# Score visits of three pieces in a PE-bound attention and MLP kernel: two single PSUM banks serve as a third strip

## The chip, the cores and the metric

The kernel runs on one core of one Trainium2 chip. The metric is the device time in microseconds of one execution. Of the core's engines five matter here: TensorE (PE), VectorE (DVE), ScalarE (ACT), GpSimd (POOL) and SyncE (SP), which issues most of the DMAs. PE writes its results to PSUM[...]; one bank holds 512 fp32 values for each of 128 partitions. ACT and DVE read PSUM; before PE may write a bank again, its reader has to be done.

## The reference

Causal attention with 16 beacon keys in front, and then an MLP with squared ReLU on the joined heads. B = 8 batches, H = 8 heads, S = 576 tokens, D = 64; d_model = 512, d_ff = 2048.

```python
k_all = concat([beacon_k, k], axis=2);  v_all = concat([beacon_v, v], axis=2)   # 16 + 576 keys
scores = q @ k_all.T / sqrt(64)          # a later key (not a beacon) is masked
a = softmax(scores)                      # + 1e-9 in the denominator
attn = a @ v_all                         # B, H, S, D
x = attn.transpose(0, 2, 1, 3).reshape(4608, 512)
h = x @ w_in;  g = relu(h) ** 2;  out = g @ w_out
```

## The kernel before

**Attention.** Heads are worked on in pairs, four pairs in a batch. The causal scores of one pair, keys on the partitions, are laid out as a stream of 1664 columns; the four pairs of a batch make 6656 columns, cut into 13 *pieces* of 512 (`PIECES`). A piece is computed in a double-bank *strip*: one bank for the even head, one for the odd head (`emit_scores`, L611, matmuls with a 64-row contraction). One ACT instruction of 2 x 512 columns turns a strip into exponentials in `pt` (`add_exp`, L620). DVE masks the diagonal blocks of a whole pair (L689, L693). Then PE multiplies by the values (L715, 15 matmuls of 65 columns for one head: 64 values and a sum), and DVE divides by the sum (L732 takes the reciprocal, L734 multiplies) into `xn`. `xn` is transposed into `xT`, by PE in the first three batches (L782) and by DMA in the others (L765). Batch 0 is done in smaller parts; batches 1 to 7 go through `add_batch`.

**MLP.** Tokens are taken in nine chunks of 512 (`add_chunk`). The first layer is 16 groups of four 512-column matmuls (L878); ACT or DVE applies the ReLU (L894 or L896) out of PSUM, and DVE squares two groups at once (L903). The second layer makes 128 tokens at a time with 16 matmuls of 512 columns (L916); ACT or DVE copies the bank to `osb` (L316 or L318), and SP stores it.

**PSUM.** Two strips of two banks, and four single banks `ps0` to `ps3` for all else: first- and second-layer groups, L715, transposes.

**Order.** Nothing is left to a scheduler of the compiler. `Order.run` is a planner: it plays the engines forward in time with assumed durations, gives each free engine the available operation of the lowest `prio`, hands out strips and single banks from pools, and returns them when their reader has ended in its account. The instructions are then emitted in that order; semaphores are derived from what each instruction reads and writes. `gate_at` holds the visits back until enough of the MLP has been done.

**A visit** is one run of score matmuls of PE. `new_visit` opens it and `add_batch` puts two pieces into it, so a batch has seven visits: six of two pieces and one of one piece. A visit of two takes both strips.

**The last 128 tokens.** `add_last` makes the second layer of the last 128 tokens in three groups of 256, 128 and 128 output columns (L828), each with its own bank, copy and store; the last copy is of 128 columns on ACT, and ACT also issues the last store.

Of the kernel before, what the change touches and what calls it, by code (L numbers as in the profile page):

```python
# [9 lines left out]
FP32 = mybir.dt.float32  # L10
# [6 lines left out]
class Op:  # L17
# [1 line left out]

    __slots__ = ("name", "engs", "dur", "emit", "prio", "need", "users", "left", "ready",  # L20
                 "take", "give", "gate", "held", "slots", "dma", "pe_time", "behind", "followers",
                 "sync", "insts", "late")

    def __init__(self, name, engs, dur, emit, prio=0.0, deps=(), take=None, give=None,
                 gate=None, dma=0.0, pe_time=0.0, behind=(), sync=(), late=0.0):
        self.name = name
        self.late = late
        self.engs = engs if isinstance(engs, (tuple, list)) else (engs,)
        self.dur = dur
        self.emit = emit  # L30
        self.prio = prio
        self.sync = list(sync)
        self.need = list(deps) + self.sync
        self.users = []
        self.take = (*take, 1)[:3] if take else None
        self.give = give
        self.gate = gate
        self.held = None
        self.slots = []
        self.dma = dma  # L40
        self.pe_time = pe_time
        self.behind = list(behind)
        self.followers = []


class Order:
# [3 lines left out]
    LAT = {"PE": 0.2, "ACT": 0.2, "DVE": 0.15, "POOL": 0.25, "SP": 0.1, "-": 0.0}  # L50

    FILL_UNTIL = 22.0
    DEPTH = {"SP": 4, "ACT": 8, "POOL": 8}
    DMA_LAT = {"SP": 0.6, "ACT": 0.6, "POOL": 2.0}

# [13 lines left out]
    def run(self):  # L69
# [24 lines left out]
        while events:  # L94
            now = events[0][0]
            while events and events[0][0] <= now + 1e-9:
                _, _, kind, op = heapq.heappop(events)
                if kind in ("done", "done_pe"):
                    for u in op.users:
                        if ("PE" in u.engs) == (kind == "done_pe"):  # L100
                            u.left -= 1
                            if u.left == 0:
                                release(u)
                elif kind == "give":
                    from_op, which = op.give if isinstance(op.give, tuple) else (op.give, 0)
                    pool, cls = from_op.take[:2]
                    self.pools[pool].append(from_op.slots[which])
                    if cls in self.inuse:
                        self.inuse[cls] -= 1
            again = True  # L110
            while again:
                again = False
                for e in engines:
                    if free[e] > now + 1e-9:
                        continue
                    best = None
                    fallback = None
                    for op in avail[e]:
                        if any(free[x] <= now + 1e-9 for x in op.engs[:op.engs.index(e)]):
                            continue  # L120
                        if op.take:
                            pool, cls, need = op.take
                            if len(self.pools[pool]) < need:
                                continue
                            if cls in self.limits and self.inuse[cls] + need > self.limits[cls]:
                                continue
                        if op.gate is not None and not op.gate(self):
                            if fallback is None or op.prio < fallback.prio:
                                fallback = op
                            continue  # L130
                        if op.dma and len(lanes[e]) >= self.DEPTH[e] and lanes[e][-self.DEPTH[e]] > now + 1e-9:
                            continue
                        if best is None or op.prio < best.prio:
                            best = op
# [17 lines left out]
                        avail[ee].remove(op)  # L152
                    if op.take:
                        pool, cls, need = op.take
                        op.slots = [self.pools[pool].pop(0) for _ in range(need)]
                        op.held = (pool, cls, op.slots[0])
                        if cls in self.inuse:
                            self.inuse[cls] += need
# [35 lines left out]
def kernel(  # L194
# [75 lines left out]
    rcp = [sb(f"rcp{i}", [128, 2 * NT], FP32) for i in range(4)]  # L270
    tri = sb("tri", [128, 4, 128], BF16)
    strips = [psum.tile([128, 2, 512], FP32, name=f"strip{i}") for i in range(2)]
    ps = [psum.tile([128, 512], FP32, name=f"ps{i}") for i in range(4)]

    def wait_for(later, first):
        tc.add_manual_dep(later.ins, first.ins.name, mybir.DependencyInfo(
# [338 lines left out]
                    start=True, stop=True,  # L615
                )

    def add_exp(name, qk, s, at, width, prio):
        def emit(e):
            nc.scalar.activation(pt[:, :, at:at + width], strips[qk.slots[s]][:, :, 0:width],  # L620
                                 AF.Exp, bias=0.0, scale=scale)

        return add(name, "ACT", 0.18 + 2 * width / 1200.0, emit, prio=prio, deps=[qk], give=(qk, s))

    exps_of = {}
    CROSS = ()
    SHIFT = 0.25
    opened = []

    def new_visit(b, n):  # L630
        pos = HP * b + 512.0 * n / PW
        parts = []

        def emit(e):
            for s, (bb, m) in enumerate(parts):
                emit_scores(bb, PIECES[m], strips[qk.slots[s]])

        qk = add(f"qk{b}.{n}", "PE", 0.2, emit, prio=100.0 * pos - 1000.0, take=("strip", "strip"), gate=gate_at(pos - SHIFT))
        opened.append((qk, parts))

    def add_batch(b):
        for pr in range(HP):
            p = HP * b + pr
            qk_ops[p], av_ops[p], exps_of[p] = [], [], []
        for n in range(NPC):
            if not opened:
                new_visit(b, n)
            qk, parts = opened[0]
            parts.append((b, n))
            qk.take = ("strip", "strip", len(parts))  # L650
            qk.dur += sum(t1 - t0 for _, _, t0, t1, _ in PIECES[n]) / 2400.0
            pairs = sorted({mm[0] for mm in PIECES[n]})
            e = add_exp(f"exp{b}.{n}", qk, len(parts) - 1, 512 * n, 512,
                        1.0e-2 * (HP * b + 512.0 * n / PW) - 30.0)
            for pr in pairs:
                p = HP * b + pr
                for o in deps_of(b, pr, 0) + av_ops[p - HP]:
                    if o not in qk.need:
                        qk.need.append(o)
                qk_ops[p].append(qk)  # L660
                exps_of[p].append(e)
            if len(parts) == 2 or n == NPC - 1 and b not in CROSS:
                opened.clear()
        for pr in range(HP):
            add_phase(b, pr, HP * b + pr, 0, WHOLE[pr][0], 100.0 * (HP * b + pr), exps_of[HP * b + pr])

    def add_pair(b, pr):
        p = HP * b + pr
        qk_ops[p], av_ops[p] = [], []
        for n, ph in enumerate(SPLIT):  # L670
            base = 20.0 * RANK.index((p, n))
            exps = []
            for i, (mms, off, width) in enumerate(ph.pieces):
# [3 lines left out]
                qk = box["qk"] = add(f"qk{p}.{n}.{i}", "PE", 0.2 + sum(max(96, mm[2] - mm[1]) for mm in mms) / 2400.0, emit_qk,  # L677
                                     prio=base + i - 1000.0, deps=deps_of(b, pr, n), take=("strip", "strip"))
                qk_ops[p].append(qk)
                exps.append(add_exp(f"exp{p}.{n}.{i}", qk, 0, PW * p + off, width, (base + i) * 1.0e-4 - 400.0))  # L680
            add_phase(b, pr, p, n, ph, base, exps)

    def add_phase(b, pr, p, n, ph, base, exps):
# [133 lines left out]
                    in_=moe_w_out.rearrange("(c p) f -> p c f", p=128)[:, i * n:(i + 1) * n, :])]  # L817
            w_ops["out", i] = add(f"wout{i}", "POOL", 1.3, emit, prio=-90 + i, behind=[v_loads[1][4]] if i == 0 else [w_ops["out", i - 1]], dma=2.6)

    def add_last(j, ts, base, sq):  # L820
        u = 2 * NCH - 1
        for n, (lo, hi) in enumerate(((0, 256), (256, 384), (384, 512))):
            prev, box = None, {}
            for qd in range(4):
                def emit_s2(e, qd=qd, lo=lo, hi=hi, box=box):
                    o = ps[box["s2"].held[2]][:, 0:hi - lo]
                    for fc in range(4 * qd, 4 * qd + 4):
                        nc.tensor.matmul(o, G_of(j)[:, fc, ts * 128:(ts + 1) * 128],  # L828
                                         w_out_sb[:, fc, lo:hi], start=(fc == 0), stop=(fc == NFT - 1))

                prev = add(f"s2.{j}.{ts}.{qd}.{n}", "PE", 0.865 * (hi - lo) / 512, emit_s2,
                           prio=base + 100 + 4 * ts + n + 0.1 * qd,
                           deps=sq[2 * qd] + sq[2 * qd + 1] + [w_ops["out", qd]], behind=[o for o in (prev or s2_ops.get((j, ts)),) if o],
                           take=None if qd else ("ps", "mlp"), pe_time=0.865 * (hi - lo) / 512)
                box.setdefault("s2", prev)
            s2_ops[j, ts] = prev
            e_ = ("ACT", "DVE", "ACT")[n]

            def emit_ev(e, lo=lo, hi=hi, box=box):
                copy_on(e, osb[u % 2][:, ts % 2, lo:hi], ps[box["s2"].held[2]][:, 0:hi - lo])  # L840

            ev = add(f"ev{j}.{ts}.{n}", e_, 0.15 + (hi - lo) / 1100.0, emit_ev, prio=-15.0, deps=[prev] + st_ops[u - 2], give=box["s2"])

            def emit_st(e, n=n, lo=lo, hi=hi):
                t0 = u * 256 + 128 * (ts % 2)
                (nc.sync, nc.sync, nc.scalar)[n].dma_start(out=out[t0:t0 + 128, lo:hi], in_=osb[u % 2][:, ts % 2, lo:hi])

            st_ops[u].append(add(f"st{j}.{ts}.{n}", ("SP", "SP", "ACT")[n], 0.65, emit_st, prio=-20.0, deps=[ev], dma=0.2))

    def G_of(j):  # L850
        return g[j % 2]

    def add_chunk(j):
        base = 1.0e5 + 1000.0 * j
        G = g[j % 2]
# [49 lines left out]
                sqs.append(add(f"sq{j}.{f}.{n}", "DVE", 0.1 + 0.6 * N / TCH, emit_sq, prio=-10.0, deps=relus))  # L905
            sq.append(sqs)
        for ts in range(TCH // 128):
            if j == NCH - 1 and ts == TCH // 128 - 1:
                add_last(j, ts, base, sq)
                continue  # L910
            prev, first = None, {}
            for qd in range(4):
                def emit_s2(e, ts=ts, qd=qd, first=first):
# [134 lines left out]
```

The softmax here doesn't subtract the row's maximum and nothing guards it: scores larger than these inputs give would overflow.

## Time and profile before

| | us |
|---|---|
| median of 3 runs (lowest to highest) | 341.09 (340.71 to 342.69) |
| profiled execution, its own time | 342.69 |
| its span, first to last instruction | 341.0 |
| PE busy | 335.6 |
| ACT busy | 190.3 |
| DVE busy | 173.0 |
| POOL busy | 92.5 |
| HBM traffic | 37.22 MB read, 9.44 MB written |

The granted TensorE clock was full (1.00) throughout. The profile is one execution; its span leaves out 1.7 us of the execution's own time around the first and last instruction. A row of PE covers a pipelined matmul with a modelled end, so rows overlap: the spacing of the starts tells what a matmul costs, not the length of its row. PE's attention work ends at 263 us or so; after that only the MLP is left.

### The profile page before, as it was taken

The numbers are of one execution on the slowest core, as the hardware profiler recorded it, in microseconds if no ns is written. First come the engines' busy times: TensorE is split into PE (matmuls) and PEld (weight loads), VectorE is DVE, ScalarE is ACT, GpSimd is POOL, SyncE is SP. The second block draws the span as 40 slices with busy tenths as digits, with TensorE's granted clock in tenths as the row PEclk, the third lists the DMA queues.
The fourth block names the chain that finished last, engine by engine and source line by source line (L and its number), as shares of the span: only waits on it lengthen the run. The fifth ranks groups of instructions, "written<-read, shape, count | busy, mean of one in ns | idle before, by whom it ended". The sixth has DMA issues, their size and how long they took to land.

```text
span 341.0 us, 7787 instructions
## 1 busy us (share of the span) xinstructions
PE 335.6 (98%) x3197; PEld 187.4 (55%) x3197; DVE 173.0 (51%) x389; ACT 190.3 (56%) x270; POOL 92.5 (27%) x145
## 2 busy tenths in 40 slices
PE   8999999999999999999999999999999999999996
PEld 7677665544564555555467855545454544444444
DVE  3886886238465982477336743767255502401400
ACT  2886765367647765576456653675367316514721
POOL 9773712406504533042315041504000000000000
PEclk9999999999999999999999999999999999999999
DMA  8999987999999999799989998997310131011003
GB/s 143 209 185 213 209 149 165 224 241 217 170 204 238 219 172 189 162 238 188 201 154 220 226 215 131 217 233 125 105 62 2 29 104 62 0 60 65 0 2 123
DMA packets 143953, 51.72 MB, mean 152 GB/s; under 512 B 130702, under 2 KB 138798, under 8 KB 143918
## 3 DMA queue, kind: packets, MB, share of 16 engines
q1 hardware_dynamic: 135375, 42.19, 61.8%
q0 software_dynamic: 7904, 8.69, 15.0%
q8 instruction: 25, 0.41, 0.5%
q10 hardware_dynamic: 639, 0.36, 0.4%
q14 instruction: 10, 0.08, 0.1%
HBM read 37.22 MB, written 9.44 MB: 137 GB/s over the span
## 4 chain that ended last, share of the span: by engine, by line
PE 97%; DVE 1%; issue 0%; ACT 0%; DVEq 0%
PE ps L878 36%; PE ps L916 36%; PE ps L715 9%; PE strip L611 9%; PE ps L286 3%; PE ps L475 2%; PE ps L782 1%; PE ps L828 1%; DVE g L903 1%; PE ps L472 0%; ACT g L894 0%; PE ps L420 0%; DVE g L896 0%; ACT osb L316 0%; DVE g L292 0%
## 5 line engine op out<-in xcount | busy, mean ns | idle before, releaser
L878 PE MATMUL ps<-xT,w_in 128*128 128x512 bf16 (+3 forms) x704 | 134.0, 340 | 0.7 <-DVE g L896 0.7
L916 PE MATMUL ps<-w_out,g 128*128 128x512 bf16 x560 | 131.4, 379 | 0.0
L620 ACT ACTIVATE pt<-strip 128x1024 bf16<-128x1024 f32 (+3 forms) x107 | 101.9, 1000 | 43.2 <-PE strip L611 42.8
L878 PEld LDWEIGHTS <-w_in 128*128 128x128 bf16 x704 | 65.5, 98 | 52.9 <-issue 2.0
L894 ACT ACTIVATE g<-ps 128x512 bf16<-128x512 f32 (+2 forms) x120 | 67.5, 563 | 45.2 <-PE ps L878 44.7
L903 DVE TENSOR_TENSOR g<-g 128x1024 bf16<-128x1024 bf16 (+2 forms) x80 | 54.2, 684 | 68.6 <-ACT g L894 67.7
L916 PEld LDWEIGHTS <-g 128*128 128x128 bf16 x560 | 51.0, 98 | 54.8 <-issue 1.7
L318 POOL CAST qk_area<-stg 128x512 bf16<-128x512 f32 (+2 forms) x60 | 40.1, 676 | 66.1 <-DMA stg<-in_q_dram 33.7
L318 POOL CAST vb<-stg 128x512 bf16<-128x512 f32 (+1 forms) x40 | 26.4, 671 | 67.8 <-DMA stg<-in_v_dram 49.3
L316 ACT COPY osb<-ps 128x512 f32<-128x512 f32 (+2 forms) x28 | 15.8, 567 | 50.8 <-PE ps L916 48.6
L715 PEld LDWEIGHTS <-pt 128*128 128x128 bf16 (+1 forms) x960 | 35.7, 98 | 11.0 <-issue 2.1
L715 PE MATMUL ps<-vb,pt 128*128 128x65 bf16 (+1 forms) x960 | 39.8, 194 | 0.0
L689 DVE TENSOR_TENSOR pt<-pt,tri 128x512 bf16<-128x512 bf16 x64 | 31.6, 503 | 10.2 <-ACT pt L620 9.0
L611 PE MATMUL strip<-qT,kT 64*128 64x208 bf16 (+15 forms) x596 | 34.2, 239 | 0.0
L734 DVE TENSOR_TENSOR xn<-ps,rcp 128x320 bf16<-128x320 f32 (+2 forms) x64 | 31.5, 492 | 2.3
L611 PEld LDWEIGHTS <-kT 64*128 64x128 bf16 x596 | 19.0, 94 | 21.2 <-issue 19.9
L732 DVE RECIPROCAL rcp<-ps 128x5 f32<-128x5 f32 (+2 forms) x64 | 12.2, 190 | 34.5 <-PE ps L715 34.2
L896 DVE TENSOR_SCALAR g<-ps 128x512 bf16<-128x512 f32 (+2 forms) x40 | 23.4, 601 | 8.6 <-PE ps L878 7.4
L318 DVE COPY osb<-ps 128x512 f32<-128x512 f32 (+1 forms) x10 | 6.5, 651 | 31.0 <-PE ps L916 19.0
L286 PE MATMUL ps<-g 128*128 128x256 bf16 (+1 forms) x83 | 12.0, 302 | 1.1 <-DVE warm L293 1.1
L362 POOL DMA_DIRECT2D stg<-in_v_dram x10 | 8.6, 866 | 6.4 <-DMA w_in<-in_moe_w_in_dram 5.3
L286 PEld LDWEIGHTS <-g 128*128 128x128 bf16 x83 | 7.9, 122 | 3.5 <-issue 1.5
(40 smaller groups left out, 82.2 us busy)
## 6 DMA issues: line engine op xcount, KB each, us to landing
out_dram<-osb SPq DMA_DIRECT2D x17, 512.0 KB, 4.3
stg<-in_q_dram SPq DMA_DIRECT2D x24, 256.0 KB, 5.0
stg<-in_k_dram SPq DMA_DIRECT2D x18, 256.0 KB, 5.3
stg<-in_v_dram SPq DMA_DIRECT2D x18, 256.0 KB, 4.7
w_in<-in_moe_w_in_dram POOLq DMA_DIRECT2D x4, 512.0 KB, 8.7
w_out<-in_moe_w_out_dram POOLq DMA_DIRECT2D x4, 512.0 KB, 11.2
stg<-in_v_dram POOLq DMA_DIRECT2D x6, 256.0 KB, 8.3
stg<-in_k_dram SPq DMA_DIRECT2D x6, 224.0 KB, 4.1
```

The lines of the kernel that those rows point to most:

```text
L286: nc.tensor.matmul(ps[bank][:, 0:cols], g[1][:, 0, 0:128], g[1][:, 0, 0:cols], start=True, stop=True)
L318: eng[e].tensor_copy(dst, src)
L611: nc.tensor.matmul(st[:, hj, at:at + t1 - t0], kT[b % 2][hp, pr, 128 * c:128 * c + 128], qT[b % 2][hp, pr, t0:t1], start=True, stop=True,)
L620: nc.scalar.activation(pt[:, :, at:at + width], strips[qk.slots[s]][:, :, 0:width], AF.Exp, bias=0.0, scale=scale)
L689: nc.vector.tensor_tensor(out=d, in0=d, in1=tri[:, m0:m0 + m, :][:, None].to_broadcast([128, 2, m, 128]), op=ALU.min)
L715: nc.tensor.matmul(a[:, at + (t - tl[0]) * (D + 1):at + (t - tl[0] + 1) * (D + 1)], P[0:rr, hj, o:o + 128], vb[b % 2][0:rr, c, 2 * pr + hj ...
L734: nc.vector.tensor_tensor(out=xn[b % 2].rearrange("p t (h d) -> p h t d", d=D)[:, h0:h0 + nh, tl[0]:tl[0] + nt], in0=a[:, :, :, 0:D], in1= ...
L878: nc.tensor.matmul(h[:, lo - spans[0][0]:hi - spans[0][0]], w_in_sb[:, mc, ft * 128:(ft + 1) * 128], xT[:, mc, lo % RING:lo % RING + hi - lo],
L894: nc.scalar.activation(dst, h, AF.Relu, bias=0.0, scale=1.0)
L896: nc.vector.tensor_scalar(out=dst, in0=h, scalar1=0.0, scalar2=None, op0=ALU.max)
L903: nc.vector.tensor_tensor(out=d, in0=d, in1=d, op=ALU.mult)
L916: nc.tensor.matmul(o, G[:, fc, ts * 128:(ts + 1) * 128], w_out_sb[:, fc, :], start=(fc == 0), stop=(fc == NFT - 1))
```

## The change

There are two parts. First, the plan of visits: batches 1 and 2 keep six visits of two pieces and one of one; batches 3 to 7 get visits of 2, 3, 3, 3 and 2 pieces. For a third strip, `ps0` and `ps1` become the two halves of one double-bank tile `strip2`. A visit of three takes the two strips and this pair, and its first piece goes to the pair. While such a visit is due (its gate is open and both strips are free), the planner holds the pair back from other work. Each piece is now an operation of its own, so that its exp is planned from the end of the piece and not from the end of the visit. Second, `add_last` and its call go away: the last 128 tokens are made like all others, 16 matmuls of 512 columns, one copy, one store on SP.

```diff
@@ Order.run
+                    if from_op.slots[which] == 2 and pool == "strip":
+                        self.pools["ps"] += self.PAIR
+                        continue
...
+                    held = ()
+                    if e == "PE" and any(o.wide and len(self.pools["strip"]) == 2 and o.gate(self) for o in avail[e]):
+                        held = self.PAIR
...
-                            if len(self.pools[pool]) < need:
+                            if len([x for x in self.pools[pool] if pool != "ps" or x not in held]) < need:
+                                continue
+                            if op.wide and not all(x in self.pools["ps"] for x in self.PAIR):
                                 continue
...
-                        op.slots = [self.pools[pool].pop(0) for _ in range(need)]
+                        op.slots = [x for x in self.pools[pool] if pool != "ps" or x not in held][:need]
+                        self.pools[pool] = [x for x in self.pools[pool] if x not in op.slots]
+                        if op.wide:
+                            op.slots.insert(0, 2)
+                            self.pools["ps"] = [x for x in self.pools["ps"] if x not in self.PAIR]
@@ PSUM
-    ps = [psum.tile([128, 512], FP32, name=f"ps{i}") for i in range(4)]
+    strips.append(psum.tile([128, 2, 512], FP32, name="strip2"))
+    ps = [strips[2][:, 0, :], strips[2][:, 1, :]] + [psum.tile([128, 512], FP32, name=f"ps{i}") for i in (2, 3)]
@@ add_batch
-        for n in range(NPC):
-            if not opened:
-                new_visit(b, n)
-            qk, parts = opened[0]
-            parts.append((b, n))
-            qk.take = ("strip", "strip", len(parts))
...
+    PLAN = ((2,2,2,2,2,2,1),(2,2,2,2,2,2,1),(2,3,3,3,2),(2,3,3,3,2),(2,3,3,3,2),(2,3,3,3,2),(2,3,3,3,2))
...
+        for size in (PLAN[b - 1] if isinstance(PLAN[0], tuple) else PLAN):
+            pos = HP * b + 512.0 * n / PW
+            box = {}
+            for s in range(size):
+                def emit(e, s=s, n=n + s, box=box):
+                    emit_scores(b, PIECES[n], strips[box["qk"].slots[s]])
+
+                qk = add(f"qk{b}.{n + s}", "PE", (0.0 if 0 < s < size - 1 else 0.1) + 512 / 2400.0, emit,
+                         prio=-1.0e6 if s else 100.0 * pos - 1000.0, behind=[qk] if s else last_qk[-1:],
+                         take=None if s else ("strip", "strip", min(size, 2)), gate=None if s else gate_at(pos - SHIFT))
...
@@ add_chunk
-            if j == NCH - 1 and ts == TCH // 128 - 1:
-                add_last(j, ts, base, sq)
-                continue
```

In the changed kernel the lines stand elsewhere: L626 for L611 (scores), L635 for L620 (exp), L725 for L715 (values), L742 and L744 for L732 and L734 (normalisation), L792 for L782 (transposes of `xn`), L490 for L475 (transposes of q and k), L855 for L878 and L890 for L916 (the two layers), L871 and L873 for L894 and L896 (ReLU), L880 for L903 (square), L331 and L333 for L316 and L318 (copies).

More of the change, by code (lines that the diff above doesn't have):

```diff
@@ L21 @@
                  "take", "give", "gate", "held", "slots", "dma", "pe_time", "behind", "followers",
-                 "sync", "insts", "late")
+                 "sync", "insts", "late", "wide")
     def __init__(self, name, engs, dur, emit, prio=0.0, deps=(), take=None, give=None,
@@ L27, in __init__ @@
         self.late = late
+        self.wide = False
         self.engs = engs if isinstance(engs, (tuple, list)) else (engs,)
@@ L52 @@
     FILL_UNTIL = 22.0
+    PAIR = [0, 1]
     DEPTH = {"SP": 4, "ACT": 8, "POOL": 8}
@@ L616, in emit_scores, with add_exp @@
                 )
-    def add_exp(name, qk, s, at, width, prio):
+    def add_exp(name, qk, s, at, width, prio, done):
         def emit(e):
@@ L621, in emit @@
                                  AF.Exp, bias=0.0, scale=scale)
-        return add(name, "ACT", 0.18 + 2 * width / 1200.0, emit, prio=prio, deps=[qk], give=(qk, s))
+        return add(name, "ACT", 0.18 + 2 * width / 1200.0, emit, prio=prio, deps=[done], give=(qk, s))
     exps_of = {}
-    CROSS = ()
     SHIFT = 0.25
[L628 to L639, printed above, removed]
+    PLAN = ((2,2,2,2,2,2,1),(2,2,2,2,2,2,1),(2,3,3,3,2),(2,3,3,3,2),(2,3,3,3,2),(2,3,3,3,2),(2,3,3,3,2))
+    last_qk = []
     def add_batch(b):
@@ L644, in add_batch @@
             qk_ops[p], av_ops[p], exps_of[p] = [], [], []
-        for n in range(NPC):
-            if not opened:
-                new_visit(b, n)
-            qk, parts = opened[0]
-            parts.append((b, n))
-            qk.take = ("strip", "strip", len(parts))
[L651 to L663, printed above, removed]
+        n = 0
+        for size in (PLAN[b - 1] if isinstance(PLAN[0], tuple) else PLAN):
[7 more added lines that the diff above has]
+                         take=None if s else ("strip", "strip", min(size, 2)), gate=None if s else gate_at(pos - SHIFT))
+                last_qk.append(qk)
+                if s == 0:
+                    qk.wide = size == 3
+                    box["qk"] = qk
+                e = add_exp(f"exp{b}.{n + s}", box["qk"], s, 512 * (n + s), 512, 1.0e-2 * (pos + 0.1 * s) - 30.0, qk)
+                for pr in sorted({mm[0] for mm in PIECES[n + s]}):
+                    p = HP * b + pr
+                    for o in deps_of(b, pr, 0) + av_ops[p - HP]:
+                        if o not in box["qk"].need:
+                            box["qk"].need.append(o)
+                    qk_ops[p].append(qk)
+                    exps_of[p].append(e)
+            n += size
+        assert n == NPC
         for pr in range(HP):
@@ L679, in add_pair @@
                 qk_ops[p].append(qk)
-                exps.append(add_exp(f"exp{p}.{n}.{i}", qk, 0, PW * p + off, width, (base + i) * 1.0e-4 - 400.0))
+                exps.append(add_exp(f"exp{p}.{n}.{i}", qk, 0, PW * p + off, width, (base + i) * 1.0e-4 - 400.0, qk))
             add_phase(b, pr, p, n, ph, base, exps)
@@ L818, in add_weights_out @@
             w_ops["out", i] = add(f"wout{i}", "POOL", 1.3, emit, prio=-90 + i, behind=[v_loads[1][4]] if i == 0 else [w_ops["out", i - 1]], dma=2.6)
[L820 to L851, printed above, removed]
     def add_chunk(j):
```

## The prediction

> **What bounds the kernel now.** I read the page first (shares, chain), then the waits, then PE's timeline, then the groups with shapes kept apart, and last the end of the timeline.
>
> ```profile
> span 341.0 us, 7787 instructions
> ...
> PE 335.6 (98%) x3197; PEld 187.4 (55%) x3197; DVE 173.0 (51%) x389; ACT 190.3 (56%) x270; POOL 92.5 (27%) x145
> ...
> PE 97%; DVE 1%; issue 0%; ACT 0%; DVEq 0%
> ```
>
> PE is busy for 98% of the span and is 97% of the chain that ended last. Its rows are modelled and overlap, so I looked for idle time in the waits:
>
> ```profile
> ACT g L894 <- PE ps L878: 44.7, 104, 2.0
> ACT pt L620 <- PE strip L611: 42.8, 27, 4.0
> ...
> DVE rcp L732 <- PE ps L715: 34.2, 34, 4.1
> ...
> PE ps L878 <- DVE g L896: 0.7, 1, 0.7
> ...
> PE ps L475 <- ACT g L894: 0.5, 1, 0.5
> ```
>
> The columns are total, times, longest. ACT and DVE wait for PE a hundred times, PE for them hardly ever. From 34 us to the last matmul only three PE gaps exceed the pure issue spacing, 1.2 us together (0.85 at 41.3, 0.19 at 63.9, 0.13 at 102.5). So the time is the sum of PE's issue spacings: whatever shortens PE's own stream is gained, and every new PE wait is lost in full.
>
> ```profile
> 149.28 2.54 PE L878 MATMUL ps<-xT,w_in 128*128 128x512 bf16 x11
> 151.75 0.61 PE L611 MATMUL strip<-qT,kT 64*128 64x208 bf16 x10
> 152.30 0.63 PE L715 MATMUL ps<-vb,pt 128*128 128x65 bf16 x15
> 152.76 1.03 PE L878 MATMUL ps<-xT,w_in 128*128 128x512 bf16 x4
> ...
> 157.63 0.40 PE L611 MATMUL strip<-qT,kT 64*128 64x96 bf16 x8
> 157.97 0.82 PE L878 MATMUL ps<-xT,w_in 128*128 128x512 bf16 x3
> ```
>
> Read the starts. Eleven 512-column matmuls at 216 ns fill 2.376 us, to 151.66; the visit starts at 151.75, 96 ns later. Its two pieces take 0.427 us of columns, yet the next kind starts 0.545 us on: some 93 ns to get out again, the rest spacing. The one-piece visit at 157.63 takes 0.33. Between L715 and L878 there is no such toll (15 x 29 ns, then on).
>
> **The Trainium skill.** "TensorEngine Tiling (Array Packing)", Key Properties, says that changing the tiling mode drains TensorE; the trace agrees and prices it: 96 ns in, 93 ns out. "TensorE: Matmul & The Clock Gate", Back-to-back issue gap, gives an isolated gap of N/2.4 + 2.5 ns, 216 at N = 512: the trace agrees. "PSUM — Partial Sum Buffer", PSUM bank collisions raise a hardware error, says to guard PSUM by bank; in the kernel before, each PSUM wait of PE is on its own bank's reader. The same page, Engine vs sequencer instructions, says that ScalarE's and VectorE's queues are strict FIFO, so one of them that waits holds back all behind it; no run here shows yet what that costs.
>
> **The change, part by part.**
>
> *Visits.* The built order of the changed program has 55 score visits for 65; PE's changes between the 64-row, 64-column and full forms fall from 145 to 123 (20 by ten visits fewer, 2 because two runs of transposes of batch 1 join). 22 x 0.0945 = 2.1 us less. Each visit dropped also saves some 15 ns of spacing (0.33 + 0.096 for a one-piece visit, against 0.216 for a piece more: 0.21, of which 0.19 is toll), 0.15 in all. The pieces, their columns and exps stay.
>
> *The last 128 tokens.* 48 matmuls (16 of 256 columns, 32 of 128) become 16 of 512: 32 x 2.5 ns = 0.1 us less on PE. After the last matmul it is the reverse:
>
> ```profile
> 335.55 2.39 PE L828 MATMUL ps<-w_out,g 128*128 128x256 bf16 x36
> ...
> 337.98 0.27 ACT L316 COPY osb<-ps 128x128 f32<-128x128 f32 x1 [1.32 <-PE ps L828]
> 338.27 0.37 ACTq L846 DMA_DIRECT2D out_dram<-osb  x1
> ```
> ```profile
> out_dram<-osb SPq DMA_DIRECT2D x1, 256.0 KB, 2.1
> ...
> out_dram<-osb ACTq DMA_DIRECT2D x1, 64.0 KB, 1.6
> ```
>
> The last copy grows from 0.27 to the 0.59 of a 512-column one (ACT does it), the landing from 1.6 to 2.1, and SP issues it: +0.9 with the hand-over. Nothing hides it.
>
> Up to here: -2.1 - 0.15 - 0.1 + 0.9 = -1.5 us.
>
> *The shared pair.* The diff makes the first two single banks the halves of one tile, `strip2`. I traced each wait of the changed program to the instruction that satisfies it. The two halves are kept apart no longer: of the readers of one half, 54 wait for PE's latest write to the other half (19 of ACT's relus on the first half wait for a first-layer write to the second; 14 of DVE's normalisations wait for a matmul of either layer there), and some 56 first waits of PE's writes on one half are for a reader of the other. Before: none of either kind. The planner, which hands the halves out as two free banks, knows nothing of it. So PE meets waits that nobody placed. Their price:
>
> ```profile
> L894 ACT ACTIVATE g<-ps 128x512 bf16<-128x512 f32 x101 | 60.3, 597 | 39.5 <-PE ps L878 39.5
> L316 ACT COPY osb<-ps 128x512 f32<-128x512 f32 x26 | 15.2, 586 | 49.5 <-PE ps L916 48.6 <-ACT pt L620 0.9
> ```
> ```profile
> L734 DVE TENSOR_TENSOR xn<-ps,rcp 128x320 bf16<-128x320 f32 x56 | 27.5, 492 | 2.0
> L896 DVE TENSOR_SCALAR g<-ps 128x512 bf16<-128x512 f32 x27 | 18.4, 687 | 7.8 <-PE ps L878 6.9
> L732 DVE RECIPROCAL rcp<-ps 128x5 f32<-128x5 f32 x56 | 10.7, 191 | 33.4 <-PE ps L715 33.2
> ```
>
> A reader starts 0.20 us after PE's last column (at the end above: PE's row ends at 337.94, modelled 0.166 past the last column, and ACT starts 0.04 later), and PE restarts about 0.05 after it. So a write on one half needs 0.20 + 0.60 + 0.05 = 0.85 us after the write that a relu waits for, 0.20 + 0.19 + 0.49 + 0.05 = 0.93 where it is a normalisation. An example, in PE time of the new order: at 83.33 15 L715 matmuls fill the second half (0.44 us), five transposes follow, and at 84.02 the next 15 go to the first half. They wait for the normalisation of the second: columns ended at 83.77, so 0.25 us is there and 0.93 is needed, 0.7 short. At 86.2 transposes need a normalisation of the first half, which has had to wait for four L916 matmuls on the second, ended just then: 0.9 short. Behind a waiting relu or normalisation queue exps, masks and squares, which later PE work needs.
>
> I did this for all of PE's waits: the new order on PE time with the spacings above, the reader's queue counted back up to 13 instructions by the rows' durations, a shortfall already paid between the two PE places taken off. Done over the order of before it gives 1.0 us, 0.2 of it after 21 us. For the new order:
>
> - to 21 us: 1.1, against 0.8 before; a further 0.9 falls on warm-up matmuls, which fill a wait for loads anyway: +0.3
> - 21 to 34 us (batch 1's transposes and first-layer groups of 240 and 272 columns): 2.9
> - 34 to 100 us: 4.0
> - 100 to 180 us: 1.6
> - 180 to 258 us: 3.6; after it, with no attention left, nothing
>
> Together 12.4, less 0.2: 12.2 us. Of this 6.3 lies in places where the other half was written at most 1.6 us of PE time ahead: nothing can hide these. The other 5.9 comes through queues of 4 to 13 instructions, surest to be misjudged. PE's present idle (1.2 after 34 us, and 0.64 at 30.2) may coincide with a new wait: 0 to 1.5 off; I take 1.2. What I left out, DVE's squares and masks that wait for ACT, and those waits that a late ACT passes on, is not shown before; it costs from nothing to some 5 us (as much again as the queued part); I take nothing. Bounds: 6.3 - 1.5 = 4.8 and 12.2 + 0.9 + 5 = 18. Value: 11.0.
>
> *The hold.* While a three-piece visit is due and both strips are free, only the other two banks are handed out, and the visit then keeps the pair until its first exp (1.02 us on ACT) ends. In the order this shows as L878 or L916 groups alternating on two banks; their shortfalls are in the sums above.
>
> Sum: -1.5 + 11.0 = +9.5 us. The profiled execution took 342.69 for a span of 341.0; it should come to about 352.2, its span to 350.5. Against the median of 341.09, 350.6.
>
> **Rivals.**
> 1. *The forecast*: shared waits stall PE by some 11 us, 350.6; its own range 347 to 354. For it: the waits are in the program, and PE has no slack. Against: half the sum runs through queues.
> 2. *Only the near waits bite*: ACT (56%) and DVE (51%) catch up, so 4.8 remain: 341.1 - 1.5 + 4.8 = 344.4. For it: their idle time before PE's results is over 100 us. Against: they idle at other moments.
> 3. *It cascades*: late exps and squares make PE wait at visits and at L916 too: 18 - 1.5, 357.6. For it: strict queues, two banks during a visit. Against: in the page before, the slack of strips is large.
> 4. *Not slower*: each shared wait finds its reader done, as PE's waits do today, and only the -1.5 is left: 339.6. This decides once the pair's two halves are on average over 0.95 us of PE work apart. For it: the rotation over four banks gives 1.7 us between neighbours in plain first-layer runs. Against: the normalisations, whose banks follow each other directly.
> That the visits do not become fewer is ruled out by the order.
>
> **How the numbers follow.** A measurement of this kernel can tell about 1% (3.4 us) from no change. Chances: forecast 0.72, near only 0.12, cascade 0.10, not slower 0.06. The range 345 to 357.5 leaves out the fourth, half of the second and a part of the third, some 0.18. Faster by over 1% needs 337.7, beyond the fourth's price: 0.01. Within 1%: most of the fourth and half of the second, 0.11. Slower: 0.88.
>
> **What would show it.** Right: PE's waits list L855, L725 or L792 behind ACT and DVE, a good 10 us in sum with 2 us or more before 34 us; the chain shows ACT and DVE shares; 55 visits with entries and exits of 96 and 93 ns; from the last matmul to the end some 3.9 us for 3.1. Wrong: PE idle under 5 us, or shared waits met with idle at strips instead, or a gap after 258 us.

## The result and the profile after

The changed kernel takes 350.17 us in the median of four runs (349.52 to 350.27); the kernel before 341.16. The ratio of the runs is 1.0252, 95% interval 1.0218 to 1.0286: 9.0 us slower by the medians, 8.6 by the ratio. The forecast was 350.6. The profiled execution took 350.19 for a span of 348.5. (The profiled execution of before, 342.69, is the slowest of that kernel's runs here, so the two spans differ by 7.5 only.)

The page of the changed kernel, shares and chain:

```profile
span 348.5 us, 7730 instructions
...
PE 335.6 (96%) x3165; PEld 188.1 (54%) x3165; DVE 167.2 (48%) x386; ACT 186.3 (53%) x271; POOL 93.4 (27%) x145
...
PE 89%; DVE 6%; ACT 3%; issue 2%; ACTq 0%; DVEq 0%
```

PE's busy time is that of before, in a span 7.5 us longer. What has changed is the chain: DVE and ACT, 1% and 0% of it before, now carry 9%. The waits say through which tile (total, times, longest):

```profile
ACT g L871 <- PE strip L855: 27.2, 27, 1.9
...
DVE rcp L742 <- PE strip L855: 6.1, 9, 1.6
DVE g L873 <- PE strip L855: 6.1, 8, 1.6
DVE rcp L742 <- PE strip L890: 5.0, 4, 2.1
...
PEld L792 <- DVE xn L744: 2.6, 4, 1.3
...
PE strip L725 <- DVE xn L744: 1.9, 4, 0.8
```

`L742 <- PE strip L855` and `L742 <- PE strip L890` are the lines to see. L742 takes the reciprocal of sums that L725 has made; it has no use for a result of either MLP layer. It waits because the other half of its tile is being written, 13 times, 11.1 us. The last two lines are the other end: PE itself behind a normalisation.

This is one such chain in the timeline, the place worked out in the prediction:

```profile
92.83 1.94 ACT L635 ACTIVATE pt<-strip 128x1024 bf16<-128x1024 f32 x2 [0.93 <-PE strip L626]
...
93.84 0.61 PE L725 MATMUL strip<-vb,pt 128*128 128x65 bf16 x15 [0.83 <-DVE xn L744]
...
94.29 0.42 PE L792 MATMUL ps<-ident,xn 112*128 112x112 bf16 x5
94.49 0.20 DVE L742 RECIPROCAL rcp<-strip 128x5 f32<-128x5 f32 x1 [0.70 <-PE strip L725]
...
94.72 0.49 DVE L744 TENSOR_TENSOR xn<-strip,rcp 128x320 bf16<-128x320 f32 x1
...
95.26 0.62 PE L725 MATMUL strip<-vb,pt 128*128 128x65 bf16 x15 [0.55 <-DVE xn L744]
...
95.72 1.03 PE L890 MATMUL ps<-w_out,g 128*128 128x512 bf16 x4
96.58 1.03 PE L890 MATMUL strip<-w_out,g 128*128 128x512 bf16 x4
97.65 0.20 DVE L742 RECIPROCAL rcp<-strip 128x5 f32<-128x5 f32 x1 [2.07 <-PE strip L890]
97.88 0.49 DVE L744 TENSOR_TENSOR xn<-strip,rcp 128x320 bf16<-128x320 f32 x1
98.28 0.75 DVE L699 TENSOR_TENSOR pt<-pt,tri 128x512 bf16<-128x512 bf16 x2
...
98.43 0.43 PE L792 MATMUL ps<-ident,xn 112*128 112x112 bf16 x5 [0.82 <-DVE xn L744]
```

At 93.84 PE fills one half. The five transposes are issued within 0.25 us; then the next L725 needs the other half, which is free, but starts only at 95.26, 0.04 after L744 has read the first: 0.71 us lost by the starts, where 0.7 was worked out. (The bracket says 0.55, since it counts from the modelled end of the row before.) At 97.65 the reciprocal starts, after four L890 matmuls on the other half; VectorE has been idle for 2.07 us. The transposes that need its result start at 98.43, 0.98 us after the last column of those four at 97.44; 0.9 was worked out. The masks of 98.28 (L699) had their last exp at 94.77: they stood behind the waiting reciprocal in VectorE's queue.

PE's idle time, read in both traces from the starts of its rows against the issue spacing (gaps over 40 ns), by stage; the limits of after are those of before moved by the delay so far:

| stage, us of before | before | after | grown by | prediction |
|---|---|---|---|---|
| 0 to 21 | 0.4 | 1.1 | 0.7 | 0.3 |
| 21 to 34 | 0.7 | 2.3 | 1.6 | 2.9 |
| 34 to 100 | 1.3 | 5.1 | 3.8 | 4.0, less 0.2 |
| 100 to 180 | 0 | 1.2 | 1.2 | 1.6 |
| 180 to 263 | 0 | 1.7 | 1.7 | 3.6 |
| sum | 2.5 | 11.6 | 9.1 | 11.0, with 1.2 taken off for overlap |

The warm-up matmuls are not in the table. The column of before is that of one execution. `tail_again` below has the same order up to the last 128 tokens, and after 21 us its trace shows 0.3 us in this way, at 61.9 and 100.4; the gaps of 0.54 at 30.9, 0.20 at 35.5 and 0.85 at 42.3, 1.6 of the 2.0 us that before shows after 21, are not in it. The last L715 starts at 268.16 before, and its like at 273.33 after, so the attention work ends there and not at the 263 us given above; no gap follows it in either trace.

The end:

```profile
342.64 1.24 PE L890 MATMUL strip<-w_out,g 128*128 128x512 bf16 x5
343.97 1.07 ACT L331 COPY osb<-strip 128x512 f32<-128x512 f32 x2 [6.31 <-PE strip L890]
344.58 0.84 SPq L916 DMA_DIRECT2D out_dram<-osb  x2
```

From the last column of the last matmul to the end of the span it takes 4.76 us, before 3.18. Both last copies stand behind the last matmul: that of tokens 256 to 383 of the chunk was ready 16 x 0.216 = 3.5 us before, but its bank is one half of the pair and the last group was being written into the other (PE's last 32 matmuls, from 336.81 on, all go to the pair).

### The profile page after: what moved, and what is told of

It reads as the page before. It is cut to its first block, busy times and chain, and to the rows that moved or that the text cites. A ratio compares the mean times of both kernels' runs of the same rounds, so it can differ in the third digit from the quotient of the medians.

```text
span 348.5 us, 7730 instructions
## 1 busy us (share of the span) xinstructions
PE 335.6 (96%) x3165; PEld 188.1 (54%) x3165; DVE 167.2 (48%) x386; ACT 186.3 (53%) x271; POOL 93.4 (27%) x145
## 4 chain that ended last, share of the span: by engine, by line
PE 89%; DVE 6%; ACT 3%; issue 2%; ACTq 0%; DVEq 0%
PE ps L890 23%; PE strip L855 17%; PE ps L855 17%; PE strip L890 12%; PE strip L626 7%; PE strip L725 4%; PE ps L725 3%; DVE xn L744 2%; PE ps L301 2%; ACT g L871 2%; DVE pt L699 1%; PE strip L301 1%; DVE rcp L742 1%; DVE g L873 1%; PE strip L792 1%
## 5 line engine op out<-in xcount | busy, mean ns | idle before, releaser
L635 ACT ACTIVATE pt<-strip 128x1024 bf16<-128x1024 f32 (+3 forms) x107 | 100.8, 1004 | 34.8 <-PE strip L626 34.4
L855 PEld LDWEIGHTS <-w_in 128*128 128x128 bf16 x704 | 65.8, 98 | 54.0 <-issue 4.0
L890 PE MATMUL ps<-w_out,g 128*128 128x512 bf16 x384 | 92.5, 379 | 0.0
L890 PEld LDWEIGHTS <-g 128*128 128x128 bf16 x576 | 53.4, 98 | 61.3 <-issue 2.6
L880 DVE TENSOR_TENSOR g<-g 128x1024 bf16<-128x1024 bf16 (+2 forms) x80 | 51.4, 653 | 70.6 <-ACT g L871 70.0
L855 PE MATMUL ps<-xT,w_in 128*128 128x512 bf16 (+3 forms) x376 | 75.0, 339 | 0.0
L855 PE MATMUL strip<-xT,w_in 128*128 128x512 bf16 (+3 forms) x328 | 67.0, 341 | 3.0 <-ACT xT L331 0.9
L333 POOL CAST qk_area<-stg 128x512 bf16<-128x512 f32 (+2 forms) x60 | 42.3, 712 | 64.3 <-DMA stg<-in_k_dram 43.6
L871 ACT ACTIVATE g<-strip 128x512 bf16<-128x512 f32 (+2 forms) x56 | 28.7, 550 | 38.8 <-PE strip L855 27.2
L333 POOL CAST vb<-stg 128x512 bf16<-128x512 f32 (+1 forms) x40 | 25.1, 636 | 78.0 <-DMA stg<-in_v_dram 77.5
L890 PE MATMUL strip<-w_out,g 128*128 128x512 bf16 x192 | 45.8, 379 | 0.0
L871 ACT ACTIVATE g<-ps 128x512 bf16<-128x512 f32 (+2 forms) x65 | 37.0, 573 | 15.0 <-PE ps L855 14.4
L725 PEld LDWEIGHTS <-pt 128*128 128x128 bf16 (+1 forms) x960 | 36.7, 97 | 13.5 <-issue 3.9
L699 DVE TENSOR_TENSOR pt<-pt,tri 128x512 bf16<-128x512 bf16 x64 | 30.7, 488 | 16.1 <-ACT pt L635 14.6
L626 PE MATMUL strip<-qT,kT 64*128 64x208 bf16 (+15 forms) x596 | 32.5, 239 | 0.3 <-ACT g L871 0.3
L626 PEld LDWEIGHTS <-kT 64*128 64x128 bf16 x596 | 19.5, 94 | 16.1 <-issue 14.3
L331 ACT COPY osb<-ps 128x512 f32<-128x512 f32 x16 | 9.4, 587 | 27.3 <-PE ps L890 14.3
L725 PE MATMUL strip<-vb,pt 128*128 128x65 bf16 (+1 forms) x507 | 21.2, 194 | 2.1 <-DVE xn L744 1.9
L331 ACT COPY osb<-strip 128x512 f32<-128x512 f32 x11 | 6.2, 588 | 25.0 <-PE strip L890 25.0
L725 PE MATMUL ps<-vb,pt 128*128 128x65 bf16 (+1 forms) x453 | 18.6, 193 | 0.0
L744 DVE TENSOR_TENSOR xn<-strip,rcp 128x320 bf16<-128x320 f32 (+2 forms) x35 | 17.1, 487 | 1.3
L333 DVE COPY osb<-ps 128x512 f32<-128x512 f32 x8 | 5.5, 691 | 21.9 <-PE ps L890 21.9
```

The lines of the kernel that those rows point to most:

```text
L331: nc.scalar.copy(dst, src)
L333: eng[e].tensor_copy(dst, src)
L626: nc.tensor.matmul(st[:, hj, at:at + t1 - t0], kT[b % 2][hp, pr, 128 * c:128 * c + 128], qT[b % 2][hp, pr, t0:t1], start=True, stop=True,)
L699: nc.vector.tensor_tensor(out=d, in0=d, in1=tri[:, m0:m0 + m, :][:, None].to_broadcast([128, 2, m, 128]), op=ALU.min)
L725: nc.tensor.matmul(a[:, at + (t - tl[0]) * (D + 1):at + (t - tl[0] + 1) * (D + 1)], P[0:rr, hj, o:o + 128], vb[b % 2][0:rr, c, 2 * pr + hj ...
L744: nc.vector.tensor_tensor(out=xn[b % 2].rearrange("p t (h d) -> p h t d", d=D)[:, h0:h0 + nh, tl[0]:tl[0] + nt], in0=a[:, :, :, 0:D], in1= ...
```

## The experiments

Each kernel was timed beside the kernel before, which had medians of 340.75, 341.04 and 340.67 us in the three sets. Each result gives the median, the ratio to before with its 95% interval, and the difference of the medians.

**Sharing alone** (`shared_only`). The kernel before, with two banks made halves of one tile:

```diff
-    ps = [psum.tile([128, 512], FP32, name=f"ps{i}") for i in range(4)]
+    strips.append(psum.tile([128, 2, 512], FP32, name="strip2"))
+    ps = [strips[2][:, 0, :], strips[2][:, 1, :]] + [psum.tile([128, 512], FP32, name=f"ps{i}") for i in (2, 3)]
```

> The kernel before, with one edit: ps0 and ps1 are the two halves of one tile that nothing else uses. PE's order, visits and the last 128 tokens stay as before. If the pair's shared waits make the loss: counted as in the prediction (spacings and row durations of before, each PE wait's shortfall), this order's waits come to 13.7 us against 1.4 for the order of before, so some 9 to 12 us more: 350 to 353. If three-piece visits, the hold on the pair or the long last copy make it: no change, 341.

352.94 us, 1.0358 (1.0345 to 1.0372), 12.2 slower. Not one instruction differs in kind or order from before. Its chain:

```profile
PE 86%; DVE 7%; ACT 3%; issue 1%; SPq 1%; DMA 1%; DVEq 0%; ACTq 0%
```

and its waits:

```profile
DVE rcp L733 <- PE strip L917: 10.7, 8, 2.1
...
PE strip L917 <- DVE g L897: 1.4, 2, 1.0
...
PE strip L917 <- DVE xn L735: 1.0, 3, 0.4
```

The same picture as in the changed kernel, without any visit of three pieces: the tile is enough. The count fits: 13.7 less the 1.4 of before is 12.3, measured 12.2. In the changed kernel the same count came out too high; why it fits here and not there I have not settled.

**No sharing, all else kept** (`unshared`). The changed kernel with two tiles again, and two exps where the third strip is read:

```diff
-    strips.append(psum.tile([128, 2, 512], FP32, name="strip2"))
-    ps = [strips[2][:, 0, :], strips[2][:, 1, :]] + [psum.tile([128, 512], FP32, name=f"ps{i}") for i in (2, 3)]
+    ps = [psum.tile([128, 512], FP32, name=f"ps{i}") for i in range(4)]
...
+            if qk.slots[s] == 2:
+                for hj in range(2):
+                    nc.scalar.activation(pt[:, hj, at:at + width], ps[hj][:, 0:width],
+                                         AF.Exp, bias=0.0, scale=scale)
+                return
```

> The changed kernel with ps0 and ps1 as two tiles again; the exp of the third strip becomes two ACT instructions of 512 columns, one for each bank. PE's order is that of the changed kernel to the instruction. If the shared waits make the loss: no shortfall is left beyond that of before, so what remains is the saving of 2.3 us and the longer end of 0.9: 339.6 for 341.1. If the three-piece visits or the hold on the pair make it: still near 350, or above, since ACT has 15 instructions more (some 0.2 us each).

339.45 us, 0.9965 (0.9952 to 0.9978), 1.3 faster. The visits of three, the hold and the order are those of the changed kernel; the 30 half exps have rows of 0.60 us and keep ACT busy for 16.3:

```profile
L639 ACT ACTIVATE pt<-ps 128x512 bf16<-128x512 f32 x30 | 16.3, 596 | 7.4 <-PE ps L628 6.2 <-issue 1.3
```

Against the changed kernel (1.0252 / 0.9965) this is 2.9%, 9.8 us (10.3 by the medians): what the sharing costs there.

**The last 128 tokens alone** (`tail_only` and `tail_again`). The kernel before without the division:

```diff
-            if j == NCH - 1 and ts == TCH // 128 - 1:
-                add_last(j, ts, base, sq)
-                continue
```

> The kernel before without the division of the last 128 tokens; four separate banks, visits of two. The prediction's terms: 0.1 us less on PE, 0.9 more after it: 341.9 for 341.1. If the whole of the 1.5 us by which the time from the last matmul to the end grew in the changed kernel belongs to this edit alone: 342.5. If part of it is a copy that waited for the other half: only the 0.8.

342.51 us, 1.0051 (1.0039 to 1.0063), 1.8 slower. From the last column to the end: 4.08 us for 3.18, so 0.9 as worked out. The other 0.9 lies elsewhere, where no instruction differs. The same program again:

> The kernel before, the last 128 tokens undivided, as in tail_only, which took 1.76 us more than before where the end accounts for 0.9 and its profiled execution showed PE behind a late transposing DMA of kT. If that DMA's lateness comes and goes: 341.6 to 342.0, some 0.9 over before. If the edit shifts the loads in a lasting way: 342.5 again.

342.37 us, 1.0045 (1.0024 to 1.0066), 1.7 slower, the runs spread from 341.22 to 343.58. The median lies where the second forecast puts it. The profiled execution took 341.44, with the same 4.08 us at the end. The two profiled executions are 1.43 us apart. First `tail_only`, then `tail_again`:

```profile
5.25 2.49 PE L286 MATMUL ps<-g 128*128 128x256 bf16 x15
...
229.43 0.61 PE L611 MATMUL strip<-qT,kT 64*128 64x112 bf16 x10 [0.42 <-DMA kT<-qk_area]
```
```profile
5.13 1.81 PE L286 MATMUL ps<-g 128*128 128x256 bf16 x15
```

These 15 are warm-up matmuls. In `tail_only` they start 0.21 us apart until 6.7 us and 0.11 from there on, in `tail_again` 0.11 apart nearly from the first, and the row after them starts at 7.57 and at 6.78: 0.8 us. The rest is 0.49 us (by the starts) behind a late transposing DMA of `kT` in `tail_only`, and 0.21 behind a mask at 185.8. Besides, the execution's own time exceeds the span by 2.0 to 2.2 us in every run of the two, by 1.7 to 1.8 in before, some 0.35 more. So the 0.9 of the end is shown, and 0.35 lies outside the span. The 0.6 that is left would be the slow warm-up and late loads, if they come more often here than in before; that is not shown, since before's profiled execution has the slow warm-up too, until 6.9 us. Why is open.

**Visits of three without sharing, and the end as before** (`unshared_last`). `unshared` with `add_last` put back:

> As unshared (separate banks, three-piece visits, two exps for the third strip), with the last 128 tokens divided as in the kernel before. If the visits save what was worked out, 2.1 us of toll and 0.15 of spacing, and nothing else changes: 338.9 for 341.1. If the visits' saving is eaten by later exps or by the hold: 341 or more.

338.60 us, 0.9947 (0.9930 to 0.9964), 2.15 faster (1.2 to 2.4 by the interval), the lowest median of all kernels here. Worked out: 2.25.

**The plan alone** (`twos`). The same with the plan of before:

```diff
-    PLAN = ((2,2,2,2,2,2,1),(2,2,2,2,2,2,1),(2,3,3,3,2),(2,3,3,3,2),(2,3,3,3,2),(2,3,3,3,2),(2,3,3,3,2))
+    PLAN = ((2,2,2,2,2,2,1),)*7
```

> As unshared_last, but with the plan of before (six visits of two, one of one) in all batches; each piece is still its own operation in the planner's account. 65 visits and 143 changes of form for 65 and 145. If unshared_last gained its 2.15 us by fewer visits: 341, the time of before, give or take 0.5. If it gained by the planning piece by piece: 339.

341.01 us, 0.9994 (0.9981 to 1.0007): no difference that shows (from 0.6 us faster to 0.2 slower). So the gain of `unshared_last` is, as far as this can tell, that of fewer visits: the spans of the two profiled executions, 339.0 and 336.7, differ by 2.3 us.

**The toll, the other way round** (`ones`). Before with visits of one piece (`if len(parts) == 1` in place of 2):

> The kernel before with visits of one piece, in all of batches 1 to 7: 101 visits for 65 and 215 changes of form for 145. If a change of form costs the 94.5 ns read from the starts, PE needs 70 x 0.0945 = 6.6 us more: 347 to 348 for 341. If the tolls were hidden behind other work, or one drain in ten only: under 343.

348.02 us, 1.0203 (1.0176 to 1.0230), 7.0 slower for 70 more changes of form: 100 ns each (86 to 112 by the interval), for 94.5 read from the starts. If the 36 visits more cost 15 ns of spacing each besides, as the prediction has it, 92 are left. Its timeline shows the tolls one by one:

```profile
149.64 1.03 PE L878 MATMUL ps<-xT,w_in 128*128 128x512 bf16 x4
150.60 0.40 PE L611 MATMUL strip<-qT,kT 64*128 64x176 bf16 x8
150.93 1.90 PE L878 MATMUL ps<-xT,w_in 128*128 128x512 bf16 x8
```

Four matmuls at 216 ns from 149.64 end at 150.50; the visit starts at 150.60, and its 0.21 us of columns take 0.33.

**The halves set apart** (`spaced`). The changed kernel, pair made of the first and the third bank:

```diff
-    PAIR = [0, 1]
+    PAIR = [0, 2]
...
-    ps = [strips[2][:, 0, :], strips[2][:, 1, :]] + [psum.tile([128, 512], FP32, name=f"ps{i}") for i in (2, 3)]
+    ps = [psum.tile([128, 512], FP32, name=f"ps{i}") for i in range(2)]
+    ps = [strips[2][:, 0, :], ps[0], strips[2][:, 1, :], ps[1]]
```

> The changed kernel with the pair made of the first and the third of the single banks in place of the first and the second; kinds, visits and their order on PE stay the same to the instruction, only the banks of the single-bank work change. If the loss comes from direct neighbours in the rotation (one half written right after the other), most of it goes: 343 to 345. If, as counting this order's waits says (14.0 us in all, 4.6 of it before 21 us, 2.6 from 34 to 100, for 2.3 and 4.0 in the changed kernel), it is the sharing itself wherever the halves stand: no great change, 348 to 352.

350.78 us, 1.0282 (1.0258 to 1.0307): no better than the changed kernel (its interval reaches 1.0286). The distance in the rotation does not help. (The planner hands out the bank that came back first, so the halves meet anyway; that is read in the code, not measured.)

**Sharing with the end as before** (`shared_last`). The changed kernel with `add_last` put back:

> The changed kernel with the last 128 tokens divided as in the kernel before; the shared pair stays. From the last matmul's last column to the end the changed kernel's trace has 4.76 us, the kernel before 3.18, tail_only and unshared 4.08 and 4.09. If the 0.67 us above 4.09 are a copy that waits for the other half, and the rest the undivided copy and store, both go here, since the last copies leave the pair: 1.5 us less than the changed kernel, 348.6 for 350.2. If the tail has nothing to do with the pair: 0.9 less, 349.3.

348.30 us, 1.0214 (1.0196 to 1.0231), against 1.0252 some 1.3 us less than the changed kernel. The two intervals overlap, so the times alone do not show it; the traces do. The end is 3.19 us, that of before, so all of the 4.76 - 3.18 = 1.58 came from the undivided end: 0.9 by itself (4.08 and 4.09 without the pair), 0.67 through the pair. `unshared_last` has the same visits and the same end with four tiles: beside it (1.0214 / 0.9947) the sharing costs 9.1 us, 9.8 by the medians, without what it does at the end.

**Threes in all batches** (`threes_all`). `unshared_last` with `PLAN = ((2,3,3,3,2),)*7`:

> As unshared_last, with 2, 3, 3, 3, 2 in batches 1 and 2 too: 51 visits and 115 changes of form for 55 and 123. By the toll 8 x 0.0945 = 0.75 us less than unshared_last: 337.9 to 338.2 where that took 338.6. If in these two batches, where PE also transposes, the hold on two banks costs more than the toll: above 339.

339.87 us, 0.9973 (0.9955 to 0.9992), 1.2 faster. The median lies where the second forecast puts it, above 339, but the runs go from 338.2 to 342.88. The profiled execution (338.54) has two waits of PE that the one of `unshared_last` has not: 0.73 us before the visit at 89.64, whose first piece waits for a normalisation of its bank, and 0.36 before transposes at 58.14. So part of what the toll saves is lost at such places; whether they make the whole shortfall against the 2.15 us of `unshared_last` is not shown.

## Why the prediction was right

*The bound.* PE's own stream, with its waits, set the time. What was added between PE's starts (9.1 us), less what its stream lost (2.3) and with the longer end (1.6), is 8.4, for 7.5 between the spans. Of the 0.9 between them 0.6 is the warm-up, which the table leaves out: the row after the 15 matmuls starts at 7.67 in before's profiled execution and at 7.06 in the other. PE's busy time, 335.6 in both, tells nothing of it: it counts modelled ends.

*Visits.* -2.25 worked out, -2.15 measured (`unshared_last`), with `twos` at nil and `ones` at 92 to 100 ns for a change of form. The Trainium skill, "TensorEngine Tiling (Array Packing)", Key Properties, names the drain; these runs price it.

*The last 128 tokens.* +0.9 - 0.1 worked out. The 0.9 at the end was measured twice (4.08 and 4.09 us for 3.18). The step that failed is the line "after it, with no attention left, nothing": the pair works on to the last copy, and the end cost 0.67 us more by it. The median of the edit alone, 1.8 us above, is not explained fully (above).

*The rest of -1.5.* `unshared`, which has both parts and no sharing, gives -1.3.

*The shared pair.* 11.0 taken. Measured: 9.8 us between the changed kernel and `unshared`, of which 0.67 is the end, and 9.1 between `shared_last` and `unshared_last` (9.8 by the medians). So 9.1 to 9.8 stand for what was priced at 11.0. (The 9.1 of the table agrees by chance, since before's column has 1.6 us of one execution's own.) The mechanism is as told, the term was sized 1 to 2 us too high. After 21 us the changed kernel's trace has 10.3 us of idle, for 12.1 counted: 2.3 for 2.9 and 1.2 for 1.6, but 5.1 for 4.0 from 34 to 100 us, and 1.7 for 3.6 from 180 on, the stage that the count had most wrong. The prediction called the part that comes through queues of 4 to 13 instructions surest to be misjudged. That delays already paid give those queues more time to drain than the count took off is a possible reason; it is not shown. The 1.2 us taken off for PE's present idle belong to one execution: the largest part, 0.85, is missing in `tail_again`.

*Luck.* The forecast came within 0.5 us of the median, closer than its terms: the stalls were priced 1 to 2 us too high and the end 0.67 too low.

*Rival 2* (near waits only, 344.4) and *rival 3* (cascade, 357.6) are both outside the measured interval; *rival 4* is what `unshared` shows when the waits are taken away. The other rival in all this, three-piece visits or the hold as the cause, falls with `shared_only` and `unshared` together.

*What was to show it.* The chain's ACT and DVE shares came as told. PE's waits list did not: its rows behind ACT and DVE sum to a few us, not ten, since each counts from the modelled end of the row before, some 0.17 us past the last column, and short waits drop out altogether. The starts show them. The end took 4.76 us, where some 3.9 was foreseen. The sign of being wrong, a gap after 258 us, was told in PE time without waits, in which 83.33 is the place of 93.84 in the trace; in the trace the attention work ends some time after 273.33, and no gap follows.

The Trainium skill, "PSUM — Partial Sum Buffer", PSUM bank collisions raise a hardware error, says in its simple version to guard PSUM by bank; the unshared kernels do, the shared ones guard by a tile of two banks, and the runs price the difference: 9.8 us here, 12.2 in `shared_only`.

## What to carry to other kernels

When two buffers that are used apart become parts of one tile, look at which instruction satisfies each wait before looking at times: an in-order engine that waits for an unrelated write also holds back what stands behind it, and a planner that does not know of the wait cannot work around it. Price such a wait by the distance on the bounding engine between the write and the next write on the other part, against the reader's latency and length. The idea of a third strip was sound: with its two banks kept apart, and two exps in place of one, it gives 2.15 us.

## What the runs showed of the hardware

A change between 64-row score matmuls and full ones costs PE 96 ns going in and 93 coming out by the starts, and 92 to 100 on average where 70 more were put in (`ones`). A reader on ACT or DVE starts 0.20 us after the last column of the matmul it waits for (0.25 at the last copy of the changed kernel), and PE goes on 0.04 to 0.05 us after the reader's end, so that a normalisation between two PE groups needs 0.93 us. Splitting an ACT exp of 1024 columns in two costs some 0.11 us of ACT's busy time (16.3 / 15 = 1.09 for 74.1 / 76 = 0.98).
